# A fused LayerNorm, windowed attention and gated MLP kernel on one core: low parts of late weights and products with inverse sums moved from GpSimd to VectorE, casts of the first chunk and one bank's copy moved from VectorE to ScalarE

## Chip, core and metric

One core of a Trainium2 chip. The metric is the device time of one execution in microseconds; the time of a kernel is the median of several runs. Inside the core TensorE (PE) multiplies, VectorE (DVE), ScalarE (ACT) and GpSimd (POOL) work element by element, and SyncE (SP) issues the transfers. Each engine takes its own instructions in a fixed order, and an instruction that has to wait holds everything behind it on its engine.

## What is computed

Cut to what matters (S = 2048 tokens, D = 512, 32 heads of 16, a window of 256, F = 1792; float32 throughout):

```python
xn = layernorm(x)
q, k, v = split(xn @ wqkv)                         # 32 heads of 16
p = softmax(where(0 <= i - j < 256, q k^T / 4, -1e9))
s = concat_heads(p v) @ wo
h = gelu(layernorm(xn) @ w1 + b1)                  # 1792 wide
g = silu(h @ w2 + b2)
return x + s * g
```

Products of float32 matrices are made of three fast passes: each operand is split into a high part (a cast to `fp32r`) and a low part (what the cast left over), and high·high, high·low and low·high are added up in PSUM.

## The kernel before

The program runs in two large phases. The first, until about 453 us of the profiled execution, computes projections and attention; the raw outputs of attention go to a DRAM tensor `oT_d`, with the sum of each row of probabilities beside them. In its last steps the hidden layer of the first chunk of 512 tokens is computed too: pre-activations of hidden blocks 6 to 13 go to DRAM (`h_d`), blocks 2 and 3 stay on the chip (`soon`), and blocks 0 and 1 come last (`first_h`, lines 710 to 715), each in one PSUM bank that is copied to the tile `hf`.

The second phase, line 814 on, is a loop over four chunks of 512 tokens. Each chunk goes through 14 hidden blocks of 128; a block is called f below, and the first chunk takes them in the order 2, 3, 0, 1, 4, 5, 6 to 13. For each block:

- `hidden(f)`: 12 matmuls into one PSUM bank (tile `h`). In the first chunk only blocks 4 and 5 still need it.
- `activate(f)`, line 824: ScalarE applies gelu and writes `g`; `split` (line 69) makes the high part `gh` by the function it is given, and the low part `gl = g - gh` always by VectorE. Blocks 2 and 3 of the first chunk are made ahead in `activate_first`, as `g_first`.
- `project(f)`, line 838: 12 matmuls into the accumulators `acc`, in four triples; a triple takes `gh` twice and then `gl`. `gh` and `gl` have two buffers each, so those of block f are written over once `project` has finished with the block two before it.

The loop index i runs from 0 to 14: at step i come `activate` of the i-th block, then the late weights, then `project` of the block before, then side work. In the first chunk the side work is:

- Late weights (lines 854 to 856): blocks 7 to 13 of `w2` (tile `w`) and the four groups of `wo` (tile `wos`). `settle` (line 549) writes a high part by ScalarE, and a low part in place by the engine that it is given. `LATE` places 1, 2, 2, 1, 1, 1, 1, 1, 1 of the eleven at steps 1 to 9.
- Inverse sums: at step 2 the sums are fetched (`den`), at steps 4 to 7 VectorE takes the reciprocal of a quarter each, and after the fourth they go to DRAM (`rden_d`).
- Means and variances of the next chunk's tokens (`bnC`, `mvC`) at steps 6 and 7, their shift at step 9.
- `load_o(c, g)` at steps 8 to 11 loads attention outputs (`or`) and the inverse sums that belong to them, repeated over 16 rows each (tile `w` in the trace, from `rden_d`, because it takes a free corner of the `w2` tiles). At steps 9 to 12 the two are multiplied, at steps 10 to 13 the product is split into `ohl` (`split_o`).

After the 14 blocks, b2 is added to `acc`, the next chunk's tokens are transposed (`yt`), and `s = o @ wo` follows from `ohl` and `wos`, is gated and stored. Later chunks have the same loop without late weights, reciprocals and ready-made hidden blocks, and with 12 more matmuls per block.

Instructions of TensorE, VectorE, ScalarE and GpSimd stand in the order in which the code issues them. Transfers are issued by SP; in the second phase a scheduler orders them. The pool `t2` gives one of five buffers to `den`, `g`, `or` and `xo` tiles, whichever the scheduler expects to be free.

In the trace every instruction carries line 43 (`Ordered.__getattr__` issues all of them), so tiles are told apart by name, and blocks by their order.

Of the kernel before, what the change touches and what calls it, by code (L numbers as in the profile page):

```python
# [13 lines left out]
ALU = mybir.AluOpType  # L14
# [36 lines left out]
def mixer_kernel(ctx, tc, x, wqk, wv, wo, w1, b1, w2, b2, out):  # L51


    nc = SimpleNamespace(**{name: Ordered(tc, name) for name in ("tensor", "vector", "scalar", "gpsimd", "sync")})
# [14 lines left out]
    def split(dst_hi, dst_lo, src, eng=None):  # L69

        (eng or nc.scalar.copy)(dst_hi, src)
        nc.vector.tensor_sub(dst_lo, src, dst_hi.bitcast(F32))
# [86 lines left out]
    fb = [psum.tile([P, 512], F32, name=f"fb{i}") for i in range(2)]  # L159
# [373 lines left out]
    def w2_part(a, f):  # L533
        at = 1024 * (f % 7) + 512 * a
        return mlp["w2", f // 7][:, at: at + 512]

    def w_part(kind, a, f):
        return {"w1": w1_part, "w2": w2_part, "wo": lambda a, f: wos[:, a, f]}[kind](a, f)
# [10 lines left out]
    def settle(kind, f, hi_by=None, lo_by=None):  # L549

        hi, lo = w_part(kind, 0, f), w_part(kind, 1, f)
        if hi_by:
            hi_by(hi, lo.bitcast(F32))
        if lo_by:
            lo_by.tensor_tensor(lo, lo.bitcast(F32), hi.bitcast(F32), op=ALU.subtract)

    def y_steps(a, b):
        run(mlp["ln"][a:b])
# [9 lines left out]
    def hidden_mm(ps, f, k):  # L568
        kt, (a, b) = k // 3, PASSES[k % 3]
        nc.tensor.matmul(ps, w1_part(a, f)[:, P * kt: P * (kt + 1)], mlp["yy"][b][kt],  # L570
                         start=(k == 0), stop=(k == 3 * KT - 1))
# [51 lines left out]
    n, raw = raws["qk"]  # L623
    nc.gpsimd.tensor_tensor(wqs[0][:, 1], raw, wqs[0][:, 0].bitcast(F32), op=ALU.subtract)
    for j, raw in enumerate(raws["v"]):
        nc.gpsimd.tensor_tensor(wva[:, 1, 2 * j: 2 * j + 2], raw, wva[:, 0, 2 * j: 2 * j + 2].bitcast(F32),
                                op=ALU.subtract)
# [82 lines left out]
    def first_h(f):  # L710

        for k in range(3 * KT):
            hidden_mm(fb[f], f, k)
        ready[f] = t2.tile([P, 512], F32, tag="t2", name=f"hf_{f}")
        nc.vector.tensor_copy(ready[f], fb[f])

    ready = {}
    fills[16 * NQ, 0] = [(first_h, (0,))]
    at(16 * NQ, activate_first)

# [65 lines left out]
    def load_y(c):  # L786
        if c > 1:
            return load_x(c, ((mlp["yp"], "y"),), "y")
        return [load(mlp["yp"], "y", xn_d[4 * c + i], f"y_{c}_{i}") for i in range(4)]

    def fetch_sums():
        den = t2.tile([P, 512], F32, tag="t2", name="den")
        for g in range(4):
            nc.sync.dma_start(den[32 * g: 32 * g + 32], oT_d[g, :, DH].rearrange("a (c t) -> a c t", c=NCH))
        return den
# [10 lines left out]
    def split_o(c, g, raw):  # L806
        ohl = gp.tile([P, 2, 512], F32R, tag="ohl", name=f"ohl_{c}_{g}", bufs=4)
        split(ohl[:, 0], ohl[:, 1], raw, nc.vector.tensor_copy)
        return ohl
# [4 lines left out]
    for c in range(NCH):  # L814
        accs = [ps_mx.tile([P, 2, 512], F32, tag="mx", name=f"acc_{c}_{i}") for i in range(2)]
        gs, os_, hs = {}, [], {}
        made = ready if c == 0 else {}

        def hidden(f):
            hs[f] = ps_st.tile([P, 512], F32, tag="b", name=f"h_{c}_{f}")  # L820
            for k in range(3 * KT):
                hidden_mm(hs[f], f, k)

        def activate(f):
            if f in made and f in soon:
                gs[f] = made[f]
                return
            src = made[f] if f in made else hs.pop(f)
            g = src if f in made and f < 2 else t2.tile([P, 512], F32, tag="t2", name=f"g_{c}_{f}")
            nc.scalar.activation(g, src, AF.Gelu_apprx_tanh, bias=b1s[:, f: f + 1])  # L830
            gh = gp.tile([P, 512], F32R, tag="gh", name=f"gh_{c}_{f}")
            gl = gp.tile([P, 512], F32R, tag="gl", name=f"gl_{c}_{f}")
            split(gh, gl, g, nc.vector.tensor_copy)
            gs[f] = (gh, gl)

        order = [2, 3, 0, 1, 4, 5, *range(6, NF)] if c == 0 else [*range(NF)]

        def project(f):
            gh, gl = gs.pop(f)
            for i in range(4):  # L840
                acc = accs[i // 2][:, i % 2]
                sl = slice(P * i, P * (i + 1))
                for k, (a, b) in enumerate(((gh, 0), (gh, 1), (gl, 0))):
                    nc.tensor.matmul(acc, a[:, sl], w2_part(b, f), start=(f == order[0] and k == 0),
                                     stop=(f == order[-1] and k == 2))

        if c:
            hidden(0)
            hidden(1)
        late = 4 if c == 0 else 0  # L850
        for i in range(NF + 1):
            if i < NF:
                activate(order[i])
            if c == 0:
                for kind, f in late_w[LATE[i]: LATE[i + 1]]:
                    settle(kind, f, nc.scalar.copy, nc.gpsimd)
            if i >= 1:
                project(order[i - 1])
            if i + 2 < NF and order[i + 2] not in made and order[i + 2] > 1:
                hidden(order[i + 2])  # L860
            if c == 0 and i == 2:
                den = fetch_sums()
            if c == 0 and 4 <= i < 8:
                nc.vector.reciprocal(den[:, P * (i - 4): P * (i - 3)], den[:, P * (i - 4): P * (i - 3)])
                if i == 7:
                    nc.sync.dma_start(rden_d.rearrange("g a (c t) -> (g a c) t", c=NCH), den)
            if c + 1 < NCH:
                if i == (4 if c == 0 else 2):
                    mlp["y"] = load_y(c + 1)
                for k, t in enumerate((4, 9) if c else (None, 6)):  # L870
                    if t is None:
                        continue
                    if i == t:
                        mlp["ln"] = layernorm(mlp["y"], f"C{c + 1}_{k}", c == 0)
                    for back, (a, b) in enumerate(((0, 2), (2, 4), (4, 5), (5, 6), (6, 8), (8, 10))):
                        if i == t + min(back, 4 + k):
                            y_steps(a, b)
            if 10 <= i < 14:
                os_.append(split_o(c, i - 10, raw))
            if 9 <= i < 13:  # L880
                raw, rec = wanted
                nc.gpsimd.tensor_tensor(raw, raw, rec, op=ALU.mult)
            if 8 <= i < 12:
                wanted = load_o(c, i - 8)
        if c == 0:
            gated = bigp.tile([P, 2, 512], F32, tag="wa", name="gated")
        us = [accs[i // 2][:, i % 2] for i in range(4)]
        for u in us:
            nc.vector.tensor_add(u, u, b2s)

        def gate(i):
            nc.scalar.activation(gated[:, i % 2], us[i], AF.Silu)

        gate(0)
        gate(1)
        for i in range(4):
            if c + 1 < NCH and i < 2:
                for kt in range(2):
                    y_transpose(c + 1, 2 * i + kt)
            tok = 512 * c + P * i  # L900
            xt = load(t2, "t2", x[tok: tok + P, :], f"xo_{c}_{i}")
            ps = ps_st.tile([P, 512], F32, tag="b", name=f"s_{c}_{i}")
            parts = [slice(0, 512)] if c < NCH - 1 or i < 3 else [slice(0, 256), slice(256, 512)]
            for cols in parts:
                k = 0
                for g in range(4):
                    for a, b in PASSES:
                        nc.tensor.matmul(ps[:, cols], os_[g][:, a, P * i: P * (i + 1)], wos[:, b, g, cols],
                                         start=(k == 0), stop=(k == 11), skip_group_check=True)
                        k += 1  # L910
            if c < NCH - 1 or i < 3:
                nc.vector.tensor_mul(gated[:, i % 2], ps, gated[:, i % 2])
                nc.gpsimd.tensor_tensor(xt, xt, gated[:, i % 2], op=ALU.add)
                nc.sync.dma_start(out[tok: tok + P, :], xt)
            else:
                for q in range(2):
                    h = slice(256 * q, 256 * q + 256)
                    nc.vector.tensor_mul(gated[:, 1, h], ps[:, h], gated[:, 1, h])
                    nc.vector.tensor_add(xt[:, h], xt[:, h], gated[:, 1, h])
                    nc.sync.dma_start(out[tok: tok + P, h], xt[:, h])  # L920
            if i < 2:
                gate(i + 2)
# [33 lines left out]
```

## Time and profile before

| | us |
|---|---|
| median of 3 runs | 789.29 (787.99 to 789.78) |
| the profiled execution's own time | 788.93 |
| its span, first to last instruction | 787.2 |
| TensorE busy in the span | 752.4 (96%) |
| VectorE busy | 483.9 (61%) |
| ScalarE busy | 372.4 (47%) |
| GpSimd busy | 311.7 (40%) |

A line of a timeline or of the chain has the start in us from the span's beginning, the duration in us, the engine, and what it did; `out<-in` are the program's tile names; `xN` merges N instructions. In brackets stands how long the engine had been idle, and what ended that. `SPq` lines are issues of transfers, not their landing. A line of groups ends with busy time and the mean ns of one instruction. In the first chunk the order of the blocks gives each line its block: the `acc` matmuls start with `g_first` (blocks 2 and 3), then come four triples each for blocks 0, 1, 4, 5 and so on to 13, and the first `yt` transpose follows block 13.

### The profile page before, as it was taken

To read this page: it belongs to the slowest core of one execution; us is meant where nothing else is said; L and a number is where in the kernel's file an instruction comes from. 1 tells how busy PE (TensorE), PEld (TensorE's weight loads), DVE (VectorE), ACT (ScalarE), POOL (GpSimd) and SP (SyncE) were. 2 spreads that over 40 slices of the span, in tenths; PEclk is the share of its full clock that TensorE was granted. 3 is DMA by queue.
4 is the path that set the end of the run, shared out by engine and by line. 5 is a ranking of instruction groups with operands and counts; after the bars stand their busy time and mean duration, and the time that the engine had idled before them with its cause. 6 is when DMAs were issued, how large, how long until landed. Compare 5 with 4: busy or idle time off the path is not lost.

```text
span 787.2 us, 18487 instructions
## 1 busy us (share of the span) xinstructions
PE 752.4 (96%) x7420; PEld 584.8 (74%) x7420; DVE 483.9 (61%) x751; ACT 372.4 (47%) x626; POOL 311.7 (40%) x586
## 2 busy tenths in 40 slices
PE   5799999999999999999999999999999999999997
PEld 4687666666768887666666677788888888888886
DVE  5686777777777678878883558733355235532243
ACT  4643766767676666777877734321113111221111
POOL 4101665757565554767766744310112010110101
PEclk9999999999999999999999999999999999999999
DMA  8633445645446763555624282520123011210011
GB/s 272 217 75 85 109 111 130 157 109 139 110 92 213 231 217 94 131 151 138 190 88 151 81 300 82 189 87 13 54 81 116 5 41 40 82 55 13 27 54 67
DMA packets 55061, 90.46 MB, mean 115 GB/s; under 512 B 10496, under 2 KB 14848, under 8 KB 54976
## 3 DMA queue, kind: packets, MB, share of 16 engines
q1 hardware_dynamic: 54976, 89.29, 39.4%
q8 instruction: 58, 0.95, 0.5%
q14 instruction: 27, 0.22, 0.1%
HBM read 44.05 MB, written 25.95 MB: 89 GB/s over the span
## 4 chain that ended last, share of the span: by engine, by line
PE 80%; DVE 8%; ACT 5%; issue 3%; DMA 2%; POOL 1%; SPq 0%; DVEq 0%; ACTq 0%; POOLq 0%
PE acc L43 17%; PE fb L43 16%; PE h L43 15%; PE zo L43 12%; PE stb L43 7%; PE s L43 6%; PE xy L43 5%; ACT pt L43 3%; DVE xy L43 2%; DVE mt L43 2%; PE pv L43 2%; DVE xnT L43 1%; POOL pt L43 1%; PE yt L43 1%; DVE gl L43 1%
## 5 line engine op out<-in xcount | busy, mean ns | idle before, releaser
L43 POOL TENSOR_SCALAR_AFFINE_SELECT pt<-pt 128x256 f32<-128x256 f32 x480 | 195.2, 431 | 176.6 <-ACT pt L43 175.2
L43 ACT ACTIVATE pt<-stb 128x768 f32<-128x768 f32 (+1 forms) x244 | 188.6, 773 | 58.1 <-PE stb L43 48.4
L43 DVE TENSOR_REDUCE mt<-xy 128x4 f32<-128x1024 f32 (+1 forms) x128 | 152.6, 1192 | 4.4
L43 PE MATMUL acc<-w,gh 128*128 128x512 f32 x432 | 133.5, 390 | 0.3 <-DVE gh L43 0.2
L43 DVE COPY_PREDICATED xy<-upper,zo 128x512 f32<-128x512 int32 x112 | 77.6, 693 | 71.8 <-PE zo L43 69.8
L43 ACT ACTIVATE g<-h,b1s 128x512 f32<-128x512 f32 x44 | 30.3, 688 | 190.0 <-PE h L43 190.0
L43 PE MATMUL fb<-xnT,wqb 64*128 64x512 f32 (+1 forms) x696 | 117.7, 404 | 0.8 <-DVE xnT L43 0.6
L43 DVE CAST gh<-g 128x512 fp32r<-128x512 f32 x52 | 28.4, 546 | 137.6 <-PE acc L43 124.8
L43 PE MATMUL zo<-pt,vt 128*17 128x128 f32 x2880 | 103.7, 275 | 2.5 <-DVE xy L43 1.9
L43 PE MATMUL stb<-qk 64*128 64x384 f32 (+1 forms) x488 | 96.6, 392 | 7.5 <-ACT pt L43 6.0
L43 PEld LDWEIGHTS zo<-pt,vt 128*17 128x17 f32 x2880 | 67.6, 97 | 39.6 <-issue 17.9
L43 PEld LDWEIGHTS acc<-w,gh 128*128 128x128 f32 x432 | 80.8, 188 | 18.0 <-DVE gh L43 1.5
L43 PE MATMUL h<-xnT 128*128 128x512 f32 x320 | 92.0, 389 | 0.0
L43 PE MATMUL acc<-w,gl 128*128 128x512 f32 x216 | 84.6, 392 | 1.3 <-DVE gl L43 1.2
L43 PEld LDWEIGHTS stb<-qk 64*128 64x128 f32 x488 | 45.6, 183 | 52.2 <-ACT pt L43 41.2
L43 PEld LDWEIGHTS fb<-xnT,wqb 64*128 64x128 f32 (+1 forms) x696 | 65.5, 186 | 8.2 <-DVE xnT L43 0.9
L43 PEld LDWEIGHTS h<-xnT 128*128 128x128 f32 x320 | 60.1, 188 | 12.5
L43 PE MATMUL xy<-qk 64*128 64x256 f32 (+2 forms) x536 | 61.3, 302 | 4.9 <-DVE mt L43 2.3
L43 PE MATMUL h<-yh,xnT 128*128 128x512 f32 x160 | 55.7, 389 | 0.0
L43 PEld LDWEIGHTS xy<-qk 64*128 64x128 f32 x536 | 44.1, 185 | 15.6 <-DVE mt L43 6.5
L43 ACT COPY oraw<-zo 128x128 f32<-128x128 f32 x128 | 34.1, 267 | 38.3 <-PE zo L43 33.8
L43 POOL TENSOR_TENSOR or<-or,w 128x512 f32<-128x512 f32 x16 | 20.7, 1296 | 74.9 <-DMA or<-oT_d 65.6
(115 smaller groups left out, 959.9 us busy)
## 6 DMA issues: line engine op xcount, KB each, us to landing
qk<-sh SPq DMA_DIRECT2D x128, 128.0 KB
qk<-pjr SPq DMA_DIRECT2D x64, 128.0 KB
oT_d<-oraw SPq DMA_DIRECT2D x32, 256.0 KB
w_d<-in_w_dram SPq DMA_DIRECT2D x14, 512.0 KB
x<-in_x_dram SPq DMA_DIRECT2D x16, 256.0 KB
or<-oT_d SPq DMA_DIRECT2D x16, 256.0 KB
w<-rden_d SPq DMA_DIRECT2D x16, 256.0 KB
xo<-in_x_dram SPq DMA_DIRECT2D x16, 256.0 KB
```

What stands on the lines that cost most here:

```text
L43: r = issue(*args, **kwargs)
```

## The change

Four places, all in what prepares or fills the second phase:

```diff
@@ first_h
-        nc.vector.tensor_copy(ready[f], fb[f])
+        (nc.scalar.copy if f else nc.vector.tensor_copy)(ready[f], fb[f])
@@ activate
-            split(gh, gl, g, nc.vector.tensor_copy)
+            split(gh, gl, g, nc.scalar.copy if c == 0 else nc.vector.tensor_copy)
@@ late weights
-                    settle(kind, f, nc.scalar.copy, nc.gpsimd)
+                    settle(kind, f, nc.scalar.copy, nc.vector)
@@ products with inverse sums
-                nc.gpsimd.tensor_tensor(raw, raw, rec, op=ALU.mult)
+                nc.vector.tensor_mul(raw, raw, rec)
```

Block 1's bank goes to `hf` by ScalarE (block 0's stays with VectorE); the 12 high parts `gh` of the first chunk's blocks 0, 1 and 4 to 13 are written by ScalarE, each right behind its gelu; the 11 low parts of late weights and the 16 products (4 per chunk) are written by VectorE, the products ahead of the next step's `gh`/`gl`. TensorE's instructions and their order stay the same. On SP the transfers of the second phase come out in another order: in the first chunk, before: `or` 0, `or` 1, store of `rden_d`, inverse sums 0 and 1, `or` 2, inverse sums 2 and 3, inverse sums 0 of the next chunk, `or` 3. After: `or` 0, store of `rden_d`, `or` 1, inverse sums 0 and 1, `or` 2, inverse sums 2 and 3, `or` 3, inverse sums 0 of the next chunk. In `t2`, `or` 2 takes `den`'s buffer and `or` 3 that of block 10's `g`; before it was block 8's `g` and `den`'s, which had passed through block 10's `g`.

## The prediction, made before the changed kernel ran

> **What bounds the kernel now.** I read the page's shares first (TensorE is busy 96% of the span), then busy times by stretch of time, to see where TensorE is not full in the second phase, then the chain of waits there, and last each engine's timeline through that stretch.
>
> ```profile
> 495.00:500.00 5.00, 3.77 (x14) 2.39 (x14) 4.83 (x6) 2.01 (x2) 2.21 (x2) 1.00 0.48 186
> 517.00:606.00 89.00, 89.00 (x403) 73.86 (x402) 37.95 (x74) 16.60 (x25) 12.52 (x11) 1.00 0.18 60
> 606.00:695.00 89.00, 89.00 (x402) 73.92 (x401) 37.73 (x74) 16.51 (x25) 12.36 (x11) 1.00 0.14 48
> ```
>
> The columns are the stretch, its length, and busy us of TensorE, its weight loads, VectorE, ScalarE and GpSimd. In chunks 1 and 2 TensorE is busy for all of 89.00 us; nothing that other engines do faster can shorten them, and chunk 3 is a copy of them. Only the first chunk has holes: 3.77 of 5 us at 495.
>
> ```profile
> 457.30 5.69 PE L43 MATMUL acc<-w,g_first 128*128 128x512 f32 x24 [0.88 <-DVE hf L43]
> 476.43 0.61 PE L43 MATMUL acc<-w,gh 128*128 128x512 f32 x2
> 485.58 0.73 PE L43 MATMUL acc<-w,gh 128*128 128x512 f32 x2 [0.18 <-DVE gh L43]
> 491.50 0.61 PE L43 MATMUL acc<-w,gh 128*128 128x512 f32 x2
> 496.39 0.50 PE L43 MATMUL acc<-w,gl 128*128 128x512 f32 x1 [1.17 <-DVE gl L43]
> 504.81 1.03 PE L43 MATMUL yt<-ident,y 128*128 128x128 f32 x8
> 525.92 2.72 PE acc L43 x12
> ```
>
> The last line, from the chain, is a block of 12 matmuls when nothing is in its way: 2.72 us, a triple every 0.68. The first chunk has 16 blocks from 457.30 on (14 `acc`, two `h`), so 43.5 us would do, to 500.8; `yt` begins at 504.81. **4.0 us is all that there is to win there.** Block 5 is the row at 476.43, block 8 at 485.58, block 10 at 491.50; the row at 496.39 is the first `gl` of block 11.
>
> ```profile
> 482.77 0.87 DVE den L43
> 483.66 4.22 DMA rden_d<-den
> 487.90 3.58 DMA w<-rden_d
> 491.61 1.31 POOL or L43
> 494.54 1.80 DVE gl L43
> ```
>
> So the chain behind those holes is: fourth reciprocal, store of the sums, load of them, product, split. VectorE comes late to the reciprocal because some of its instructions are stretched:
>
> ```profile
> L43 DVE TENSOR_TENSOR gl<-g,gh 128x512 fp32r<-128x512 f32 x10 | 8.9, 894 | 1.0
> L43 DVE CAST gh<-g 128x512 fp32r<-128x512 f32 x10 | 6.6, 663 | 5.7 <-PE acc L43 5.7
> 456.46 0.69 DVE L43 COPY hf<-fb 128x512 f32<-128x512 f32 x1
> 457.96 1.67 DVE L43 TENSOR_TENSOR gl<-hf,gh 128x512 fp32r<-128x512 f32 x1
> 468.31 0.43 DVE L43 CAST gh<-g 128x512 fp32r<-128x512 f32 x1 [5.54 <-PE acc L43]
> 468.84 0.69 DVE L43 TENSOR_TENSOR gl<-g,gh 128x512 fp32r<-128x512 f32 x1
> 472.64 0.95 DVE L43 RECIPROCAL den<-den 128x128 f32<-128x128 f32 x1 [3.11 <-DMA y<-xn_d]
> 475.40 1.60 DVE L43 TENSOR_TENSOR gl<-g,gh 128x512 fp32r<-128x512 f32 x1
> 480.00 0.64 DVE L43 BATCH_NORM_STATS2 bnC<-y 128x6 f32<-128x512 f32 x1
> 480.77 0.66 DVE L43 BATCH_NORM_STATS2 bnC<-y 128x6 f32<-128x512 f32 x1
> 454.40 7.82 POOL L43 TENSOR_TENSOR w<-w 128x512 fp32r<-128x512 f32 x5 [4.00 <-ACT w L43]
> 473.71 4.44 POOL L43 TENSOR_TENSOR wos<-wos 128x512 fp32r<-128x512 f32 x3
> 494.52 1.27 POOL L43 TENSOR_TENSOR or<-or,w 128x512 f32<-128x512 f32 x1 [1.61 <-DMA w<-rden_d]
> 497.14 1.41 POOL L43 TENSOR_TENSOR or<-or,w 128x512 f32<-128x512 f32 x1 [1.34 <-DMA w<-rden_d]
> 502.12 1.29 POOL L43 TENSOR_TENSOR or<-or,w 128x512 f32<-128x512 f32 x1 [3.57 <-DMA w<-rden_d]
> ```
>
> A `gl` takes 0.69 alone (468.84) and 1.60 to 1.80 when it lies inside a GpSimd instruction over 128x512 (457.96, 475.40, 494.54); `gh` 0.43 alone, 0.66 on average.
>
> **The change, part by part.**
>
> *Block 1's bank by ScalarE.* TensorE waits for this copy at 457.30. VectorE takes 0.69; the nearest ScalarE row, the same shape out of a bank, 0.58:
>
> ```profile
> 448.93 0.58 ACT L43 COPY hr<-fb 128x512 f32<-128x512 f32 x1 [0.27 <-PE stb L43]
> 471.19 0.69 ACT L43 ACTIVATE g<-h,b1s 128x512 f32<-128x512 f32 x1 [4.18 <-PE h L43]
> 479.95 0.60 ACT L43 CAST wos<-wos 128x512 fp32r<-128x512 f32 x1
> ```
>
> Gain 0.1. Behind the copy on ScalarE now stand block 7's high part and block 0's gelu, which ran at about 454; they go to 457.0. ScalarE then needs 0.7 for the gelu and 0.6 for `gh`, VectorE 0.7 each for a low part and `gl`: block 0 is ready by 459.6, and TensorE wants it at 465.4. Hidden, with 6 us of cover.
>
> *`gh` by ScalarE.* VectorE loses 12 casts, ScalarE gains 12 of 0.60. A `gh` waits until `project` two blocks back is through, and now holds ScalarE: late high parts and the next gelu queue behind it. Per block ScalarE has 0.7 + 0.6 + 0.6 = 1.9 us of work against 2.72, and the late weights are wanted blocks later. `gh` is ready 0.7 after the block two back, `gl` 1.4, against 2.72: hidden as long as VectorE has nothing in front.
>
> *Low parts by VectorE.* Eleven of 0.69 in place of GpSimd's 1.3 to 1.7, and with them the stretching goes. How this moves the reciprocal: its start at 472.64 waits for a transfer and stays. Blocks 4, 5, 6, 7, 8 begin on TensorE at 473.6, 476.3, 479.0, 481.8, 484.5. Block 6's `gl` starts 0.75 after block 5 begins, at 477.05 (what ends there is block 4). Then VectorE does in a row, by start-to-start spacing in the trace: `gl` 0.62, low part 0.65, reciprocal 0.87, two means 0.80 each, `gl` 0.62, low part 0.65, reciprocal 0.87. Sum 5.9: the fourth ends at 482.95, before at 483.64; **0.7 earlier**. Two more means and block 8's `gl` end at 485.2; TensorE wants it 0.45 after 484.5 and waits 0.3. Block 9 begins at 487.5, block 10 at 490.2.
>
> *Products by VectorE.* The store of the sums took 4.22 with a load of 256 KB issued just ahead; that load now goes behind it, so 3.6 (the load of equal size, next row of the chain) to 4.22. The first inverse sums are then there, call it r, another 3.58 later: 490.1 to 490.7, I take **r = 490.4** (before 491.5). The Trainium skill, page "DMA: Bandwidth & Descriptors", section "Anatomy of one DMA", gives a fixed 2.0 us and bytes over 436 GB/s, by which I would estimate 2.6 for each of the two and r = 488.1; the trace's 4.22 and 3.58 disagree, with other transfers beside them, and the measurement decides.
>
> The product stands ahead of block 10's `gl` on VectorE, and TensorE waits for that. From r: wake-up 0.1, product 0.63, `gl` 0.69, TensorE again at r + 1.5, ten matmuls 2.27, block 11 at r + 3.7. The second sums came 2.9 behind the first (494.4 against 491.5, by GpSimd's rows): product at r + 3.0, block 11's `gl` done at r + 4.3, wanted at r + 4.2; block 12 at r + 6.6. The third came 5.5 behind: product r + 5.6, `gl` r + 6.9, in time; block 13 at r + 9.4. The fourth product waits for `or` 3:
>
> ```profile
> 489.22 0.57 SPq L43 DMA_DIRECT2D or<-oT_d  x1
> 489.84 3.67 SPq L43 DMA_DIRECT2D w<-rden_d  x3
> 493.62 0.74 SPq L43 DMA_DIRECT2D or<-oT_d  x1
> ```
>
> It was issued at 493.62 behind the next chunk's sums and used at r + 10.5. Between the third sums and it 5.0 us passed for three transfers, 1.7 each; one of them now goes behind, so r + 8.8. It needs block 10's `gl` done (r + 1.5, about 492), which the row allows. Product 0.63, `gl` 0.69: TensorE goes on at 8.8 + 0.1 + 1.32 + 0.05 = 10.3, ten matmuls, end at **r + 12.5 = 502.9**, before 504.8. Bounds: `or` 3 at r + 8.15 or sooner gives r + 12.1; as late as before, r + 14.2; with r from 490.1 to 491.5 that is 502.2 to 505.7.
>
> *Later chunks.* A product of 0.69 must fit in front of a `gh` on VectorE:
>
> ```profile
> 572.04 0.43 DVE L43 CAST gh<-g 128x512 fp32r<-128x512 f32 x1 [2.60 <-PE acc L43]
> 577.48 0.43 DVE L43 CAST gh<-g 128x512 fp32r<-128x512 f32 x1 [1.56 <-PE acc L43]
> 755.02 1.29 POOL L43 TENSOR_TENSOR or<-or,w 128x512 f32<-128x512 f32 x1 [9.81 <-DMA or<-oT_d]
> 762.18 0.69 DVE L43 TENSOR_TENSOR ohl<-or,ohl 128x512 fp32r<-128x512 f32 x1
> ```
>
> VectorE is idle 2.60 and 1.56 there, the smallest gap is twice the product. The latest data, chunk 3's at 755.02, come 7 us before its place behind the row at 762.18. Nothing; without that cover, 0.69 per product, 8 us for the twelve.
>
> **Sum.** 504.8 - 502.9 is 1.9, with 0.1 from the copy **2.0 us**. The profiled execution's own time is 788.93 (span 787.2 and 1.73 around it), so 786.9; the median shown is 0.36 higher. I give 787.1, in between. Its own range, from r and `or` 3, is a gain of 1.0 to 2.8: 786.0 to 788.3.
>
> **The rivals.**
>
> *A: no hole left.* If the sums are there by 489.2 (1.45 before the 490.65 at which block 10 wants `gl`) and `or` 3 by 497, TensorE runs through: 4.1 us, 784.8. For it: the store is alone at first. Against: 4.22 + 3.58 must shrink by 1.5. The rule quoted above would give this.
>
> *B: VectorE held by the last load, slower.* The end is `or` 3's landing + 3.74 (0.1 + 0.63 + 0.69 + 0.05 + 2.27). If the new place in the queue does not bring it forward, it lands at 502.0 as before, block 13 ends at 505.7, 0.9 later: 789.8 by its own time, 790.2 by the median; the point from which it decides is 501.1. GpSimd waited there without harm, because block 13's `gl` was not behind it. For it: 502.12 is in the trace, and `or` 3 now waits for a `gl` that stands behind a product. Against: one transfer fewer in front. The same page's section "Queues, rings and completion order" says that completions are not first in, first out per issuing engine; so being issued earlier does not promise landing earlier. The rows here landed in order of issue.
>
> *C: the hole only changes its name.* r stays at 491.5 (the store no faster, or VectorE still stretched with GpSimd gone, so that the change does not do what it says) and `or` 3 comes 9.2 after it: end 504.4, gain 0.5, 788.6.
>
> **How the numbers follow.** Forecast 0.55, A 0.10, B 0.18, C 0.17. About 0.2%, 1.6 us, is what a measurement of this kernel can tell from none. Of the forecast some three quarters lie beyond it, with A 0.51 faster; slower needs B with `or` 3 after 502.7, 0.09; the rest is same, 0.40. The range 785.0 to 789.6 leaves out about half of A and half of B.
>
> **What would show it.** Right: no `gl` of 1.6 in the first chunk; the store of the sums issued near 483.0; the first product on VectorE near 490.5, with TensorE waiting about 1.3 us for block 10's `gl`, little at 11 and 12, and about half a microsecond at 13; `yt` near 502.8; chunks 1 to 3 full. Wrong: a hole in front of block 0 or 1, `gh` waiting on a blocked ScalarE, a TensorE hole after 517, or the last product later than 501.

## The result, and the profile after

The changed kernel takes 786.43 us (median; 785.69 to 787.35) beside 789.46 us (787.99 to 790.65) for the kernel before, measured together: a ratio of 0.9962, 95% interval 0.995 to 0.9974, so 2.1 to 3.9 us less. Timed again in a later series it takes 786.50 beside 788.84, ratio 0.997 (0.9959 to 0.9982). The forecast was 787.1, its range 785.0 to 789.6. The profiled execution's own time is 786.61. One of the seven executions took 1052.88 us at a mean granted clock of 0.63; it is left out of the range and the ratio.

The page's first part, after:

```profile
span 784.9 us, 18472 instructions
PE 750.9 (96%) x7420; PEld 585.5 (75%) x7420; DVE 481.3 (61%) x765; ACT 380.4 (48%) x639; POOL 276.4 (35%) x559
```

The span is 2.3 us shorter. GpSimd lost 35 us of work, ScalarE gained 8, and VectorE's busy time fell by 2.6. TensorE does the same instructions and stays the bound, so the 2.3 us must be sought in its holes. Its busy time fell by 1.5 as well, but the ends of matmuls are modelled in the record and part of a hole counts as busy, so below the holes are read from the starts of matmuls.

Busy time by stretch (columns as in the prediction):

```profile
490.00:495.00 5.00, 3.25 (x15) 2.48 (x14) 4.27 (x8) 2.98 (x6) 0.00 (x0) 1.00 0.50 180
495.00:500.00 5.00, 5.00 (x24) 4.14 (x23) 4.54 (x9) 2.60 (x4) 0.00 (x0) 1.00 0.62 187
515.00:604.00 89.00, 89.00 (x402) 73.87 (x401) 40.12 (x78) 16.45 (x24) 7.29 (x6) 1.00 0.18 60
604.00:693.00 89.00, 89.00 (x403) 73.86 (x402) 40.12 (x78) 16.44 (x24) 7.23 (x6) 1.00 0.15 48
```

Chunks 1 and 2 are full as before. One hole is left in the first chunk, between 490 and 495. TensorE's timeline there:

```profile
456.67 5.74 PE L43 MATMUL acc<-w,g_first 128*128 128x512 f32 x24 [0.68 <-ACT hf L43]
...
484.01 0.61 PE L43 MATMUL acc<-w,gh 128*128 128x512 f32 x2
...
489.64 0.61 PE L43 MATMUL acc<-w,gh 128*128 128x512 f32 x2
492.01 0.50 PE L43 MATMUL acc<-w,gl 128*128 128x512 f32 x1 [1.75 <-DVE gl L43]
...
502.59 1.03 PE L43 MATMUL yt<-ident,y 128*128 128x128 f32 x8
```

The rows are the first `acc`, block 8, block 10, block 10's first `gl`, and `yt`. From the first `acc` to `yt` now pass 502.59 - 456.67 = 45.92 us; before it was 504.81 - 457.30 = 47.51. That is 1.59 of the 2.3. Another 0.20 is the bank's copy: the first `acc` waits for `hf` for 0.68 in place of 0.88. The attention phase, whose instructions are the same, brought the start of the last six `fb` matmuls 0.43 sooner, and what follows `yt` took 0.08 less. I ascribe neither to the change: over the executions below the first `acc` starts anywhere from 456.45 to 458.51, and the times of one kernel differ by as much (the changed one, timed again, from 785.19 to 788.77). So I compare kernels by the stretch from the first `acc` to `yt`, which needs 16 × 2.72 = 43.5 us.

The stretch splits again at block 10. Before, block 10 began 491.50 - 457.30 = 34.20 after the first `acc` and `yt` 13.31 later. After, it begins at 489.64 - 456.67 = 32.97 and `yt` comes 12.95 later. So 1.23 came from the blocks ahead of block 10 and only 0.36 from the blocks that depend on the inverse sums.

The chain of waits (start, length, what) names what made the hole at block 10:

```profile
481.43 0.87 DVE den L43
...
482.32 2.01 DMA rden_d<-den
...
484.35 6.22 DMA w<-rden_d
...
490.66 0.09 DVE or L43
...
491.27 0.69 DVE gl L43
...
492.01 10.75 PE acc L43 x46
```

It is the chain of before, with VectorE in GpSimd's place: reciprocal, store, load, product, `gl`. The store is down from 4.22 to 2.01 us, the load up from 3.58 to 6.22. SP's timeline shows what stands around them:

```profile
482.32 0.32 SPq L43 DMA_DIRECT2D rden_d<-den  x1
482.69 0.61 SPq L43 DMA_DIRECT2D or<-oT_d  x1
484.35 1.20 SPq L43 DMA_DIRECT2D w<-rden_d  x2
485.59 0.57 SPq L43 DMA_DIRECT2D or<-oT_d  x1
486.21 1.68 SPq L43 DMA_DIRECT2D w<-rden_d  x2
491.98 0.57 SPq L43 DMA_DIRECT2D or<-oT_d  x1
```

`or` 1 is issued 0.37 behind the store, and `or` 2 and the other sums while the first sums are under way. `or` 3 is issued at 491.98, 35.31 after the first `acc` (before: 36.32), now ahead of the next chunk's sums. VectorE's and ScalarE's timelines show that it lands early enough:

```profile
456.03 0.59 ACT L43 COPY hf<-fb 128x512 f32<-128x512 f32 x1 [2.66 <-DMA w<-w_d]
475.87 0.62 ACT L43 CAST gh<-g 128x512 fp32r<-128x512 f32 x1 [0.95 <-ACT g L43]
...
458.50 0.69 DVE L43 TENSOR_TENSOR gl<-hf,gh 128x512 fp32r<-128x512 f32 x1 [0.64 <-ACT gh L43]
476.52 0.69 DVE L43 TENSOR_TENSOR gl<-g,gh 128x512 fp32r<-128x512 f32 x1 [0.56 <-ACT gh L43]
490.66 0.69 DVE L43 TENSOR_TENSOR or<-or,w 128x512 f32<-128x512 f32 x1 [3.86 <-DMA w<-rden_d]
491.27 0.68 DVE L43 TENSOR_TENSOR gl<-g,gh 128x512 fp32r<-128x512 f32 x1
498.03 0.69 DVE L43 TENSOR_TENSOR or<-or,w 128x512 f32<-128x512 f32 x1 [0.27 <-DMA or<-oT_d]
```

The last product waits 0.27, and TensorE nothing. `gl` starts 0.03 behind its `gh`, and no `gl` is stretched any more. At 490.66 VectorE had stood idle for 3.86 us while block 10's `gh` was ready: the product was its next instruction, and `gl` was queued behind it.

### The profile page after: what moved, and what is told of

It is laid out like the page before. It is cut to its first block, busy times and chain, and to the rows that moved or that the text cites. A ratio compares the mean times of both kernels' runs of the same rounds, so it can differ in the third digit from the quotient of the medians.

```text
span 784.9 us, 18472 instructions
## 1 busy us (share of the span) xinstructions
PE 750.9 (96%) x7420; PEld 585.5 (75%) x7420; DVE 481.3 (61%) x765; ACT 380.4 (48%) x639; POOL 276.4 (35%) x559
## 4 chain that ended last, share of the span: by engine, by line
PE 81%; DVE 7%; ACT 4%; issue 3%; DMA 2%; POOL 1%; SPq 1%; DVEq 0%; ACTq 0%; POOLq 0%
PE acc L43 17%; PE fb L43 16%; PE h L43 15%; PE zo L43 12%; PE stb L43 7%; PE s L43 6%; PE xy L43 5%; ACT pt L43 3%; DVE xy L43 2%; DVE mt L43 2%; PE pv L43 2%; SPq L43 1%; DVE xnT L43 1%; POOL pt L43 1%; DMA w<-rden_d 1%
## 5 line engine op out<-in xcount | busy, mean ns | idle before, releaser
L43 DVE CAST gh<-g 128x512 fp32r<-128x512 f32 x42 | 17.9, 427 | 128.5 <-PE acc L43 115.8
L43 POOL TENSOR_TENSOR xo<-xo,gated 128x512 f32<-128x512 f32 x15 | 19.4, 1292 | 153.5 <-DVE gated L43 147.0
L43 POOL TENSOR_TENSOR rsC<-veC,mhalf 128x4 f32<-128x4 f32 x6 | 6.6, 1099 | 152.6 <-DVE veC L43 152.6
```

The source lines that it names most:

```text
L43: r = issue(*args, **kwargs)
```

## The experiments

All were run after the result was known. Times in the table are us after the first `acc`, from each kernel's own trace. "Holes" are what TensorE lost against 0.227 us per matmul (2.72 / 12), by the starts in its timeline, in blocks 5 to 8 and in blocks 10 to 13. In undo_casts the matmuls of block 13 lost some 1.2 more at a lower granted clock, which its 2.73 leaves out.

| kernel | store issued | first product | last product | holes, 5 to 8 | holes, 10 to 13 (block) | to `yt` |
|---|---|---|---|---|---|---|
| before | 26.36 | 34.31 | 44.82 | 1.37 | 1.82 (11), 0.53 (12) | 47.51 |
| after | 25.65 | 33.99 | 41.36 | 0.15 | 2.02 (10) | 45.92 |
| changed_again | 25.65 | 34.11 | 40.98 | 0.16 | 2.14 (10) | 46.02 |
| undo_low | 24.45 | 33.08 | 42.01 | 0.06 | 1.23 (10), 0.73 (13) | 45.76 |
| undo_products | 25.65 | 33.59 | 41.59 | 0.16 | 1.78 (11) | 45.70 |
| undo_copy | 25.61 | 33.17 | 39.98 | 0.16 | 1.23 (10) | 45.09 |
| undo_casts | 26.08 | 33.25 | 44.28 | 1.12 | 0.86 (10), 2.73 (13) | 49.82 |
| undo_casts_timed | 26.08 | 32.74 | 44.42 | 1.11 | 0.36 (10), 0.48 (11, 12), 2.94 (13) | 48.70 |
| casts_behind | 26.09 | 33.23 | 43.34 | 1.11 | 0.11 (13) | 44.97 |
| only_low | 26.06 | 32.95 | 41.95 | 1.11 | 0.62 (11), 0.38 (12), 0.35 (13) | 46.28 |
| only_casts | 24.40 | 32.55 | 44.52 | 0.07 | 1.12 (12) | 44.87 |
| behind_gl | 25.66 | 33.79 | 41.09 | 0.15 | 0.30 (11) | 44.18 |
| or_early | 25.66 | 31.41 | 38.22 | 0.15 | none | 43.87 |
| both | 25.65 | 31.52 | 39.68 | 0.15 | none | 43.84 |

**One part undone at a time.** Each of these is the changed kernel with one edit taken back; one execution each, 788.17 us for the kernel before beside them.

*undo_low:* the low parts go back to GpSimd.

```diff
-                    settle(kind, f, nc.scalar.copy, nc.vector)
+                    settle(kind, f, nc.scalar.copy, nc.gpsimd)
```

> The changed kernel, but the low parts of the late weights by GpSimd again. Measured is the stretch from TensorE's first acc matmul to the first yt transpose: 47.5 us before, 45.9 after the change, 43.5 with no hole. Theory (the gain is VectorE no longer stretched beside GpSimd, which brings the store of the sums forward): several gl take 1.6 again, the fourth reciprocal ends 0.5 to 1 us later than the 482.3 of the changed kernel (both counted from the first acc matmul), and the stretch is 46.5 to 47.5. Rival (the casts taken from VectorE are the gain): the stretch stays within 0.3 of 45.9.

Measured: 45.76 to `yt`, 786.25 us. My own theory fell and the rival held: with the casts gone from VectorE, its low parts are no help. Without them in its row the fourth reciprocal is over sooner and the store goes out 1.2 earlier than in the changed kernel, though two `gl` lie inside a GpSimd low part again:

```profile
460.64 1.35 DVE L43 TENSOR_TENSOR gl<-hf,gh 128x512 fp32r<-128x512 f32 x1 [1.63 <-ACT gh L43]
479.97 0.95 DVE L43 RECIPROCAL den<-den 128x128 f32<-128x128 f32 x1
```

*undo_products:* the products go back to GpSimd.

```diff
-                nc.vector.tensor_mul(raw, raw, rec)
+                nc.gpsimd.tensor_tensor(raw, raw, rec, op=ALU.mult)
```

> The changed kernel, but the products with inverse sums by GpSimd again. Theory (the products by VectorE only make a new hole, because block 10's gl waits behind a load): the hole of 2.0 us at block 10 goes, a smaller one comes at block 11, where gl is behind ohl, which waits for GpSimd's product; the stretch is 44.5 to 45.9. Rival (GpSimd's 1.3 us products, and the stretching by them, were part of the old hole, so moving them was part of the gain): 46.5 or more. Chunks 1 to 3 stay full in both.

Measured: 45.70 to `yt`, as expected; 788.24 us, with the first `acc` at 458.51, 1.84 later than after, which this edit does not touch. The hole at block 10 is gone and one at block 11 has come. VectorE's, GpSimd's and TensorE's timelines:

```profile
494.50 1.76 DVE L43 TENSOR_TENSOR gl<-g,gh 128x512 fp32r<-128x512 f32 x1
...
492.10 1.30 POOL L43 TENSOR_TENSOR or<-or,w 128x512 f32<-128x512 f32 x1 [3.66 <-DMA w<-rden_d]
494.34 1.38 POOL L43 TENSOR_TENSOR or<-or,w 128x512 f32<-128x512 f32 x1 [0.94 <-DMA w<-rden_d]
...
496.32 0.50 PE L43 MATMUL acc<-w,gl 128*128 128x512 f32 x1 [1.51 <-DVE gl L43]
```

With GpSimd the wait for the sums is out of VectorE's way, but block 11's `gl` begins inside the second product and takes 1.76. The two places cost about the same, so this part of the change is worth nothing that these two traces show (0.2 the other way).

*undo_copy:* block 1's bank is copied by VectorE again.

```diff
-        (nc.scalar.copy if f else nc.vector.tensor_copy)(ready[f], fb[f])
+        nc.vector.tensor_copy(ready[f], fb[f])
```

> The changed kernel, but block 1's bank copied by VectorE again. Theory: the gap in front of the first acc matmul, from the start of the last six fb matmuls to it, was 2.42 before and 2.22 after; it goes back by 0.1 to 0.2, and the stretch stays at 45.9 within 0.2. Rival (ScalarE held by this copy delays late high parts and the blocks behind): the stretch is shorter than 45.6.

Measured: the first `acc` waits 0.88 again, the 0.20 as expected, but `yt` comes 45.09 after it, 0.83 sooner than after; 785.56 us. The first sums landed 0.8 sooner, for stores issued at the same time (25.61, 25.65), and the hole at block 10 shrank by as much. The rival's number came, but not its cause: up to that load nothing is sooner (block 10 begins 32.95 after the first `acc`, against 32.97), so no block ahead of it was held by ScalarE. What differs is the load itself, 5.46 in place of 6.22, behind the same transfers. So the transfers of one execution can move the stretch by 0.8, and the differences of 0.2 between undo_low, undo_products and the changed kernel say no more than that these two parts are no clear gain.

*undo_casts:* `gh` of the first chunk goes back to VectorE.

```diff
-            split(gh, gl, g, nc.scalar.copy if c == 0 else nc.vector.tensor_copy)
+            split(gh, gl, g, nc.vector.tensor_copy)
```

> The changed kernel, but the high parts gh of the first chunk by VectorE again. Theory: VectorE has 0.53 more per block, no instruction is stretched, the fourth reciprocal ends 0.3 to 0.8 later, the stretch is 46.2 to 46.8. Rival (the casts carry the gain): 47 or more. Second rival (the casts are free, because waits for transfers decide): 45.9.

Measured: 49.82 to `yt` and 792.50 us in this one execution; the first rival's number, not the theory's. About 1.1 stands at block 8, where a `gh` is late. Most stands at block 13, as this execution's TensorE timeline shows, and then its stretches:

```profile
503.71 1.15 PE L43 MATMUL acc<-w,gh 128*128 128x512 f32 x2 [2.08 <-DVE gh L43]
508.16 1.04 PE L43 MATMUL yt<-ident,y 128*128 128x128 f32 x8
```

```profile
504.00:506.00 2.00, 2.00 (x6) 1.35 (x6) 1.48 (x3) 0.00 (x0) 0.00 (x0) 0.50 0.53 193
506.00:508.00 2.00, 2.00 (x8) 1.58 (x7) 1.35 (x2) 0.00 (x0) 0.00 (x0) 0.69 0.71 215
```

Behind a hole of 2.08 us the granted clock (the column after the five engines) was 0.50 and 0.69 for some 4 us, and block 13's matmuls took 508.16 - 503.71 = 4.45 us in place of 2.72.

**Timed again, and the product moved.** Medians of 5 to 12 executions, the kernel before at 788.84 us beside them. The first is the changed kernel itself:

> The changed kernel once more, timed beside the three others: a ratio of 0.995 to 0.9974 to the kernel before, and the stretch 45.9 within 0.3 with store and first load of the sums at 2.0 and 6.2 us. If these two differ from run to run by more than 1 us, the hole at block 10 is a matter of chance and not of the order of issue.

Measured: 786.50 us (785.19 to 788.77), ratio 0.997 (0.9959 to 0.9982); 46.02 to `yt`, with a hole marked 1.87 at block 10. The picture of the result repeats.

*behind_gl:* each product is issued one step later, behind that step's `gh` and `gl` and just ahead of its own split.

```diff
             if 10 <= i < 14:
+                raw, rec = wanted.pop(0)
+                nc.vector.tensor_mul(raw, raw, rec)
                 os_.append(split_o(c, i - 10, raw))
-            if 9 <= i < 13:
-                raw, rec = wanted
-                nc.vector.tensor_mul(raw, raw, rec)
             if 8 <= i < 12:
-                wanted = load_o(c, i - 8)
+                wanted.append(load_o(c, i - 8))
```

> The changed kernel, with each product on VectorE one place later, behind the gl of its step and just ahead of its own split into ohl. Theory (block 10's gl only waits because it stands behind the product): no hole at block 10, one of 0.3 to 0.8 at block 11, whose gl now stands behind the first product and split; the stretch from the first acc matmul to the first yt is 44.0 to 44.8 against 45.9, so 1.1 to 1.9 us faster than the changed kernel. Rival (the order on VectorE does not matter, the later loads decide anyway): 45.6 or more.

Measured: 44.18 to `yt`; 785.02 us (784.64 to 785.37), ratio 0.9951 (0.9939 to 0.9963). As the theory had it. The sums are as late as in the changed kernel (product at 33.79), but VectorE waits for them with `gl` done, and the chain of waits is TensorE almost alone. (`or` 3 is issued 3.7 sooner here, but its product comes at 41.09 against 41.36.) VectorE's timeline, then the chain:

```profile
487.38 0.69 DVE L43 TENSOR_TENSOR gl<-g,gh 128x512 fp32r<-128x512 f32 x1 [0.81 <-ACT gh L43]
490.24 0.69 DVE L43 TENSOR_TENSOR or<-or,w 128x512 f32<-128x512 f32 x1 [2.17 <-DMA w<-rden_d]
492.04 0.69 DVE L43 TENSOR_TENSOR gl<-g,gh 128x512 fp32r<-128x512 f32 x1
```

```profile
477.83 14.93 PE acc L43 x65
...
492.78 8.01 PE acc L43 x34
```

*or_early:* the four `or` loads of the first chunk go into a tile of their own at step 5, in space that is free by then, long before the store.

```diff
+            if c == 0 and i == 5:
+                first = bigp.tile([P, 4, 512], F32, tag="wa", name="or_first")
+                for g in range(4):
+                    nc.sync.dma_start(first[:, g], oT_d[g, :, 0:DH, 0:512])
...
-        raw = load(t2, "t2", oT_d[g, :, 0:DH, cols], f"or_{c}_{g}")
+        raw = first[:, g] if c == 0 else load(t2, "t2", oT_d[g, :, 0:DH, cols], f"or_{c}_{g}")
```

> The changed kernel, with the first chunk's four attention loads (or) in the free tile of g_first and issued at step 5, when hardly any transfer is under way, instead of between the store and the loads of the sums. Products stay ahead of gl. Theory (store and first load shared the queue with a load of 256 KB: 2.01 + 6.22 us, before 4.22 + 3.58): store about 2.0 and first load 3.6 to 4.2, the first sums 2.0 to 2.6 us earlier, the hole at block 10 shrinks from 2.0 to under 0.3, the stretch is 43.5 to 44.2. Rival (the load of the sums takes its 6 us by itself, or beside the other three loads of sums): the hole stays at 1.5 to 2 and the stretch at 45.5 or more.

Measured: 43.87 to `yt`; 784.80 us (784.32 to 786.62), ratio 0.9956 (0.9942 to 0.997). SP's and VectorE's timelines, then the chain:

```profile
482.12 0.32 SPq L43 DMA_DIRECT2D rden_d<-den  x1
484.09 9.60 SPq L43 DMA_DIRECT2D w<-rden_d  x7
...
487.87 0.69 DVE L43 TENSOR_TENSOR or_first<-or_first,w 128x512 f32<-128x512 f32 x1 [1.27 <-DMA w<-rden_d]
```

```profile
477.84 22.64 PE acc L43 x99
```

The store is issued as late after the first `acc` as in the changed kernel. With no `or` load beside them the store takes 484.09 - 482.12 = 1.97 and the first load 487.87 - 484.09 = 3.78. The products come in time and TensorE has no hole. So what the first load takes beyond that in the changed kernel, 2.4 us, comes from the `or` loads.

*both:* the two edits together.

> Early attention loads and products behind gl together. Theory: 43.5 to 43.8, no hole, 2.1 to 2.4 us faster than the changed kernel, 4.5 to 5.5 faster than before by medians. Rival (only one of the two waits was real): no better than the better of the two alone by 0.2.

Measured: 43.84 to `yt`; 785.60 us (784.45 to 786.14), ratio 0.9957 (0.9945 to 0.997), 3.2 us below the kernel before. Either edit alone closes the hole, and there is nothing left for the second; the time that I expected of the sum was missed. So or_early and behind_gl are the best versions found, 784.80 and 785.02 us where the changed kernel took 786.50 in the same series; the intervals of their ratios overlap that of the changed kernel.

**The casts and the low parts alone.** The kernel before took 789.33 us beside these four.

*undo_casts_timed* repeats undo_casts over ten executions.

> The changed kernel with casts by VectorE again, once more and timed, since one look alone gave 792.5 us. Theory (the order of the transfers brings the last attention load late): it repeats, 2 to 4 us slower than the kernel before, the hole at block 13 over 2 us with the granted clock at 0.5 to 0.7 behind it. Rival (a chance in the transfers of that one execution): within 1 us of the kernel before, hole under 1 us and clock 1.00.

Measured: 789.90 us (789.13 to 792.29), ratio 1.0012 (0.9999 to 1.0025): no slower than the kernel before by more than can be told. Time and clock came as the rival had them, the hole as the theory had it. Its profiled execution, at 791.34 among the slower of ten, has the hole at block 13 again, with the clock at 1.00 throughout. Its chain there:

```profile
492.97 9.71 DMA or<-oT_d
...
502.76 0.06 DVE or L43
...
503.36 0.43 DVE gh L43
...
503.89 0.70 DVE gl L43
...
504.64 2.56 PE acc L43 x10
```

With `gh` on VectorE the transfers come out in the order of before: two `or` ahead of the store, and `or` 3 behind the next chunk's sums. It lands at 502.7; the last product waits for it, and block 13's `gh` and `gl` stand behind the product.

*casts_behind:* undo_casts with behind_gl.

> The changed kernel with casts by VectorE again, and each product one place later, behind the gl of its step. Theory (the 3.9 us that the casts alone cost when undone are the last attention load, which came late and held block 13's gh and gl behind the product, and the lower clock after that hole of 2.1 us): the hole at block 13 goes, the clock stays at 1.00, the stretch is 44.5 to 45.8. Rival (VectorE simply has too much work with casts, low parts and products): 47 or more.

Measured: 44.97 to `yt`, 786.93 us in a single execution. The 1.11 at block 8 is still there, the hole at block 13 is not, though the last product comes at 43.34, after block 13 has begun. VectorE does all the work of undo_casts, so the 3 us at block 13 were the place of one waiting product and not the amount of work. The transfers helped a little: `or` 3 is issued ahead of the next chunk's sums here and used 1.0 sooner, but with the product ahead of `gl` it would still have held block 13.

*only_casts:* the kernel before with `gh` of the first chunk by ScalarE, and nothing else.

> The kernel before, with one part of the change alone: the high parts gh of the first chunk by ScalarE. Low parts, products and the bank's copy stay where they were. New theory (from the undone parts: only the casts changed the stretch, 45.8 without the low parts, 45.7 without the products, 49.8 without the casts): the stretch from the first acc matmul to the first yt is 45.3 to 46.2, the gap ahead of it 2.42 as before, and the time 1.2 to 2.2 us under the kernel before, ratio 0.997 to 0.9985. Rival (the parts only work together, since low parts and products on GpSimd stretch VectorE): 46.8 to 47.5, no faster than before.

Measured: 787.33 us (784.47 to 790.71), ratio 0.997 (0.9956 to 0.9984), the same ratio as the whole change when it was timed again. The profile is of the execution at 790.71. There `yt` comes 44.87 after the first `acc`, sooner than the 45.3 to 46.2 expected, but a hole follows one step on. GpSimd's and TensorE's timelines:

```profile
502.34 1.28 POOL L43 TENSOR_TENSOR or<-or,w 128x512 f32<-128x512 f32 x1 [5.39 <-DMA or<-oT_d]
...
508.52 1.71 PE L43 MATMUL yt<-ident,y 128*128 128x128 f32 x8 [2.06 <-DVE xnT L43]
```

`or` 3 is behind the next chunk's sums here too and lands at 502.2; the second `yt` waits 2.06 us for VectorE. The chain of waits joins the two: product, `ohl`, b2 added to `acc`, ScalarE's `gated` and `yh`, VectorE's `xnT`, `yt`. No edit tried it. Whether the other executions, up to 6 us shorter, have this hole was not seen.

*only_low:* the kernel before with the low parts by VectorE.

> The kernel before, with the low parts of the late weights by VectorE alone; casts, copy and products stay. New theory (VectorE with casts and low parts has too much ahead of the fourth reciprocal and of gh): the stretched instructions up to 490 go, but the stretch is 46.8 to 48. Rival, the recorded step of the prediction (with nothing stretched the reciprocal is 0.7 earlier, and TensorE follows): 46.0 to 46.5.

Measured: 46.28 to `yt`, 787.68 us in a single execution. The 0.57 at blocks 5 and 7 goes, but the hole at block 8 grows from 0.80 to 1.11, and the holes behind the sums shrink. The number is that of the rival; the theory that I had formed for this run fell.

## Why the prediction was right, and where its steps were off

The direction, the place and the size were right: 1.8 us of the change's own (1.59 and 0.20) stand against 2.0 forecast. That the size fits so well owes something to luck, since two errors behind the fourth reciprocal nearly cancel, as told below. The medians differ by more, 3.0 us in the first series and 2.3 in the later one; what lies beyond 1.8 no row of the traces ties to the change.

- *The bank's copy:* right, under-sized: 0.20 for 0.1.
- *`gh` by ScalarE hidden:* right. It takes 0.62, and `gl` follows it at once (476.52). Every kernel with these casts on ScalarE has 0.06 to 0.16 of holes in blocks 5 to 8; each kernel that has the low parts moved and not the casts has 1.1, at block 8.
- *VectorE relieved up to block 10:* right in number. By the prediction's sum block 10 begins 490.2 - 457.2 = 33.0 after the first `acc`; measured 32.97. The fourth reciprocal came 0.7 earlier, as forecast (the store is issued 0.71 sooner). But the reason given was not the one that carries it. The prediction credited the low parts, by the end of the stretching; undo_low has the store 1.2 earlier still without them, close to the two low parts of 0.65 that the prediction's own sum puts into VectorE's row. The casts do it: alone they bring the store 1.96 forward (only_casts), the low parts alone 0.30 (only_low), and with the casts gone the low parts only stand in VectorE's row. In the stretch the two do not add up: 44.87 and 46.28 alone, against 47.51 before and 45.92 for all four edits.
- *Store and first load, r:* this is the term that was mis-sized. The store was put at 3.6 to 4.2 and the load at 3.58; measured 2.01 and 6.22. The prediction saw that an `or` load moved behind the store, and did not see that the load of the sums, issued 1.7 behind that `or` load, would then pay for it. Instead of 33.2, r came at 490.57 - 456.67 = 33.9; the 0.7 won at the reciprocal shrank to 0.3. or_early shows it: with the `or` loads long done, 1.97 and 3.78, and the product at 31.41. It is the `or` load ahead that counts: in the kernel before, `or` 2 was issued 1.3 behind the first load and that load took 3.58 all the same. The Trainium skill's page "DMA: Bandwidth & Descriptors", section "Anatomy of one DMA", from which the prediction estimated 2.6 each, states its fixed time and rate for transfers issued by GpSimd, and SP issues these two. In or_early their sum comes out at 5.75 against 5.2, the store under the estimate and the load over it; in the changed kernel, at 8.23, it does not hold.
- *The holes behind r:* block 10 was to wait 1.3 and by the starts waited 1.9 (the row marks 1.75), for r was later. Blocks 11 and 13 were to lose 0.2 and 0.5 and lost nothing: the second product came 2.3 behind the first, not 2.9, and the last `or` was usable 7.4 after r, not 8.8 (498.03 against 490.57). The late r and the early last `or` nearly cancel: block 10 to `yt` took 12.95 where the sum has 12.7.
- *Products by VectorE:* counted as part of the gain, worth nothing by undo_products. The wait that they put ahead of `gl`, which the prediction priced at r + 1.5, is as dear as the stretching that they remove.
- *Rival A* (no hole left) did not come with the change; its condition, the sums and the last `or` early, is what or_early made, and the gain is then 47.51 - 43.87 = 3.6 in the stretch. *Rival B* is the mechanism of undo_casts: in the timed execution `or` 3 lands at 502.7, 44.3 after the first `acc` (B had 44.8), and the hole is marked 2.33. Its condition, `or` 3 not brought forward, is met when the casts go back and the transfers keep their old order. *C* was half right: r came 0.3 earlier, but the last `or` did not lag behind it.
- *Later chunks:* nothing, as said: 89.00 of 89.00 us.

## What to carry to other kernels

An instruction that waits for a transfer belongs behind the work that the bounding engine wants next, even on an engine that is mostly idle: one step later in VectorE's order was worth 1.7 us here, as much as the whole change had gained. A store and a load that follow each other on the critical path should have no other large transfer issued just ahead of either: with the `or` loads issued earlier, their 8.23 us became 5.75. Price the edits of a bundle one by one, since two that relieve the same engine do not add up: here the casts alone gave a ratio of 0.997, as all four did in the later series.

## What was not expected of the hardware

A transfer issued behind an `or` load took longer; one issued just ahead of an `or` load did not. From the issue of the store to the issue of the load that waits for it passed 3.0 to 4.2 us in the five kernels with an `or` load just ahead of the store (before, undo_casts twice, casts_behind, only_low) and 2.0 in the nine others, seven of which issue an `or` load 0.4 behind it. From the issue of the first load of the sums to the first product passed 5.5 to 6.6 us in those seven, whose `or` load stands between store and load, and 3.7 to 3.9 in the other seven, though the first five issue an `or` load 1.3 behind it. The first product so came 32.6 to 34.3 after the first `acc` in all kernels with `or` loads among the sums, although the store was issued anywhere from 24.4 to 26.4.

After a hole of 2.08 us TensorE's granted clock fell once to 0.50 and 0.69 for 4 us; in another execution of the same kernel a hole of 2.33 had no such sequel, nor had 1.75 and 1.87 in the changed kernel. What makes the difference was not found.

A small GpSimd instruction did not stretch VectorE's. In the changed kernel a low part runs inside one over 128x4 (VectorE's and GpSimd's timelines):

```profile
485.64 0.68 DVE L43 TENSOR_TENSOR wos<-wos 128x512 fp32r<-128x512 f32 x1
...
485.22 1.39 POOL L43 TENSOR_TENSOR rsC<-veC,mhalf 128x4 f32<-128x4 f32 x1 [35.23 <-DVE veC L43]
```

The low part takes 0.68, where in undo_products a `gl` that meets a product over 128x512 takes 1.76.
